# Linear attention feeding a routed expert layer: another route to 1/rms, routing logits summed on GpSimd, three routing groups for four

## Chip, cores and metric

One core of a Trainium2 chip runs the kernel. The metric is the device time of one execution in microseconds (us). TensorE does the matrix products and transposes (PE in the profile, PEld its weight loads), VectorE is DVE, ScalarE is ACT, GpSimd is POOL, and SyncE (SP) issues most loads. Each engine executes its instructions strictly in the order in which the kernel wrote them, and waits where an operand is not ready.

## What is computed

The reference, cut to what matters (q, k, v are 8 batches x 8 heads x 576 rows x 64; x is 4608 rows x 512; there are 8 experts of 512 x 1024 x 512):

```python
kv  = einsum('bhsd,bhde->...', k, v)          # one 64x64 state per batch and head
out = einsum('bhsd,bhde->bhse', q, kv)
rms = sqrt(mean(out * out, axis=-1) + 1e-06)  # per row and head
x   = (out / rms * g_norm)                    # -> (4608, 512)
do_compute = x @ w_skip > 0
logits = x[do_compute] @ w_gate; e_idx = argmax(logits)
gate_w = max softmax probability
out[do_compute] += gate_w * (relu(x @ w1[e]) @ w2[e])   # e = e_idx of the row
```

## The kernel before

There are two parts: an attention part, up to about 181 us in the trace, and an expert part after it.

**Units.** The 4608 rows are 36 tiles of 128. A *unit* is two tiles and four of the eight heads, so there are 36 units, and after unit n all of the tiles up to n are done. A batch gives four units; the ninth column of rows of four batches is collected into two more units, without a transpose of their own. Units 0 to 17 belong to batches 0 to 3 and 18 to 35 to batches 4 to 7.

**A step of the loop.** Step n of the main loop writes, in this order: `turn(n+1)` (four PE transposes of q, L287, and ACT's copy `qT` out of PSUM, L290); `values(n)` (32 matmuls into `o_ps`, L322, and ACT's Square of the result into `sq`, L327); the extra jobs of PE that are due in the step; `norm(n-1)` (DVE multiplies `o_ps` by 1/rms into `xl`, L344); `scale(n)` (DVE sums `sq` over the 64 columns into `rs`, L334, and POOL raises it to the power -1/2, L335); `finish(n-1)` (POOL multiplies by `g_norm` into `xb`, L362, and copies the nine logit columns into `lp`, L366); and the extra jobs of DVE. `o_ps` has two buffers, so `values(n+1)` waits for `xl` of unit n-1. The mean's 1/64 and the epsilon are folded into constants: `sq` has a 65th column that holds 64 times 1e-6, and `g_norm` is scaled by 8.

**The extra jobs on PE** prepare the state of a batch in the five steps ahead of its first unit: `state` twice (72 matmuls each, L219; the second ends with ACT's copy `kvn`, L226), `state_t` (transposes L235, ACT's copy `kvT` L238), `state_m` (the gating weights times the state, L246, two DVE copies L250), `state_s` (a product with a swap matrix L256, ACT's copy `kvs` L259). All use the one buffer of `kv_ps`, so the next batch's first `state` waits for `kvs`. `turn_8` (L302, two ACT copies L306) transposes the collected rows; it shares the one PSUM buffer of `turn`. With four units to a batch the steps repeat in a cycle of four, called here **A** (`state_s`, then the first `state` of the next batch), **B** (the second `state`), **C** (`turn_8`, `state_t`) and **D** (`state_m`).

**Logits.** The nine gating columns (eight experts and the skip score) are extra columns of the state, so each unit's `xl` holds 4 heads x 9 partial logits per row; a row's logits are their sum over the eight heads.

**Routing groups.** The tiles are routed in four groups that end after 8, 18, 26 and 36 tiles. For each: `choose` (DVE sums `lp` over the heads, L391, then finds the best expert, L394 to L409), `rank` (PE counts rows of equal expert, L419 to L427), `number` (DVE turns the counts into slot numbers, L436 to L447, builds one-hot rows `oha_k` of 128 columns per tile, L449, and `ohc` and `bv`, L457 and L461), and `settle` (PE, L470, and two DVE additions into `srow`, L482). Three groups are handled inside the loop, one to three steps apart; `early` then starts one indirect gather from the slots known so far. The last group of ten tiles is handled behind the loop, while PE works on the first rows of expert 0; there too ACT's `Exp` (L597) starts the chain of gate weights (L599 to L605, L457, L461, L470), which the remaining rows of expert 0 wait for.

**Expert part.** PE multiplies 384 rows per expert by w1 (L634) and w2 (L641), eight times; this takes PE alone from about 203 us to the end.

Of the kernel before, what the change touches and what calls it, by code (L numbers as in the profile page):

```python
# [7 lines left out]
FP32 = mybir.dt.float32  # L8
# [8 lines left out]
def kernel(  # L17
# [29 lines left out]
    nc = tc.nc  # L47
# [140 lines left out]
    nc.vector.tensor_copy(out=top[:, :], in_=ebase[:, :])  # L188


    sqs = [setup.tile([P, 2, 4, D + 1], FP32, name=f"sq{i}") for i in range(2)]
    for t in sqs:
        nc.vector.memset(t[:, :, :, D:D + 1], float(D * 1e-6))
    half_t = setup.tile([P, 2, 4], FP32)
    nc.vector.memset(half_t[:, :, :], -0.5)

# [75 lines left out]
    NU = len(units)  # L272
    ends = [8, 18, 26, 36]
    TG = 10

    qTs, q8s, ops, rss, lps, xbs = {}, {}, {}, {}, {}, {}

# [33 lines left out]
    def values(n):  # L311
        _, b, i, u = units[n]
        qT = qTs.pop(n)
        ps = ps_o.tile([P, 2, 512], FP32, tag="o", name="o_ps")
        for w in range(2):
            for a in range(2):
                for hf in range(2):
                    for r in range(2):
                        bb = b if i is not None else 4 * b + 2 * hf + r
                        rows = slice(r * 64, (r + 1) * 64)  # L320
                        kv = kvns[bb] if w == r else kvss[bb]
                        nc.tensor.matmul(  # L322
                            out=ps[hf * 64:(hf + 1) * 64, r, (2 * w + a) * KD:(2 * w + a + 1) * KD],
                            lhsT=qT[rows, w, hf, a * 64:(a + 1) * 64], rhs=kv[rows, a, u, :],
                            start=True, stop=True, skip_group_check=True)
        sq = sqs[n % 2]
        nc.scalar.activation(out=sq[:, :, :, 0:D], in_=heads(ps, 0, D), func=ACT.Square)  # L327
        ops[n] = (ps, sq)

    def scale(n):  # L330

        _, sq = ops[n]
        rs = att_pool.tile([P, 2, 4], FP32, tag="rs", name="rs")
        nc.vector.tensor_reduce(out=rs[:, :, :], in_=sq[:, :, :, :], axis=AX.X, op=ALU.add)  # L334
        nc.gpsimd.tensor_tensor(out=rs[:, :, :], in0=rs[:, :, :], in1=half_t[:, :, :], op=ALU.pow)  # L335
        rss[n] = rs

    def norm(n):

        nq, b, i, u = units[n]  # L340
        (ps, _), rs = ops.pop(n), rss.pop(n)
        r4 = rs[:, :, :].unsqueeze(3)
        xl = att_pool.tile([P, 2, 4, KD], FP32, tag="xl", name="xl")
        nc.vector.tensor_tensor(out=xl[:, :, :, :], in0=heads(ps, 0, KD),  # L344
# [3 lines left out]
    def finish(n, xl):  # L348
# [3 lines left out]
        if t0 == 0 and u == 0:  # L352
            lps[g] = gat_pool.tile([P, TG, H, G], FP32, tag="lp", name="lp")
        if i is None:
# [3 lines left out]
        else:  # L358
# [6 lines left out]
            in1=g_b[:, :].unsqueeze(1).unsqueeze(1).to_broadcast([P, 2, 4, D]), op=ALU.mult)  # L365
        nc.gpsimd.tensor_copy(out=lps[g][:, t0:t0 + 2, 4 * u:4 * u + 4, :], in_=xl[:, :, :, D:KD])  # L366
        if u == 0:
# [15 lines left out]

    ohbs, rks, bvs, sps = {}, {}, {}, {}

    def choose(g):
        t0, t1 = ([0] + ends)[g], ends[g]
        nt = t1 - t0
        lp = lps.pop(g)
        lg = gat_pool.tile([P, TG, G], FP32, tag="lg", name="lg")[:, 0:nt, :]  # L390
        nc.vector.tensor_reduce(out=lg, in_=lp[:, 0:nt, :, :].rearrange("p t h g -> p t g h"),  # L391
                                axis=AX.X, op=ALU.add)
        mx = gat_pool.tile([P, TG], FP32, tag="mx", name="mx")[:, 0:nt]
# [37 lines left out]
    def number(g):  # L431
# [16 lines left out]
                                       op=ALU.arith_shift_right)  # L448
        nc.vector.tensor_tensor(out=oha_k[:, t0:t1, :],  # L449
                                in0=row128_i[:, :].unsqueeze(1).to_broadcast([P, nt, P]),  # L450
                                in1=lo_i.unsqueeze(2).to_broadcast([P, nt, P]), op=ALU.is_equal)
        bvs[g] = columns(t0, nt, colid_i, row_k, 2, gat_pool)

    def columns(t0, nt, colid, val, pieces, pool):
# [104 lines left out]
    for n in range(NU + 2):  # L559
        if n + 1 < NU:  # L560
            turn(n + 1)
        if n < NU:
            values(n)
        jobs(n, "pe")
        done = norm(n - 1) if 1 <= n <= NU else None
        if n < NU:
            scale(n)
        store = done() if done else None
        if store:
            at(n + 1, "end", store)  # L570
        jobs(n, "dve")
        if n in ends[:LAST]:
# [3 lines left out]
            at(n + 1, "dve", lambda g=g: number(g))  # L576
            at(n + 2, "pe", lambda g=g: settle(g))
            at(n + 2, "dve", lambda g=g: add_pieces(srow[:, :], sps.pop(g), 2))
            if g == LAST - 1:
                at(n + 2, "dve", early)  # L580
        jobs(n, "end")
# [186 lines left out]
```

## Time and profile before

| | |
|---|---|
| runs | 547.68, 547.9, 550.95 us (median 547.9) |
| the profiled execution | 547.66 us, its span 545.9 us |
| mean granted PE clock | 0.92 |
| busy share of the span | PE 85%, DVE 23%, ACT 16%, POOL 31% |
| first Square of the loop | 29.26 us |
| last Square of the loop (unit 35) | 176.21 us |

A row of the group view reads: line, engine, operation, output <- inputs, shape, count | busy us in all, mean ns of one | idle us of that engine just before, and what ended the idling. A row of the windows view gives a stretch, its length, busy us of the engines with their instruction counts, the granted PE clock as a share of full speed, and the share of DMA. In the timeline a row gives start, duration, engine, line, operation, and in brackets the idle time before it and what ended it; in the chain of waits, start, duration, and the engine and line that time was spent on.

### The profile page before, as it was taken

How to read it: one execution, taken by the hardware profiler on the slowest of the kernel's cores; microseconds unless marked ns; L12 is line 12 of the kernel's file. 1: busy time of each engine (PE TensorE's matmuls, PEld its weight loads, DVE VectorE, ACT ScalarE, POOL GpSimd, SP SyncE). 2: the span in 40 equal slices, each digit the busy share in tenths (PEclk: the TensorE clock that was granted, in tenths of full speed). 3: DMA queues.
4: the chain of work that ended last, by engine and by line, in shares of the span. 5: the costliest groups of instructions: out<-in, count | busy, mean ns of one | idle time of the engine just before them, and what ended most of it. 6: DMA issues, size and time to landing. Idle time of an engine off the chain costs nothing.

```text
span 545.9 us, 8655 instructions
## 1 busy us (share of the span) xinstructions
PE 462.9 (85%) x3776; PEld 285.4 (52%) x3776; DVE 124.7 (23%) x265; ACT 89.8 (16%) x182; POOL 168.1 (31%) x183
## 2 busy tenths in 40 slices
PE   2477686867674789999999999999999999999990
PEld 2365565655553658455455455455445545545540
DVE  0223473383554670101101100110210210110011
ACT  0144433324332102011011011001001001101100
POOL 2038769757789467310100010010010010010010
PEclk9998958669865699999999999999999999999997
DMA  8997966779593446753241350431422000010000
GB/s 292 376 391 264 368 226 163 255 257 396 181 391 81 117 120 208 269 193 104 89 156 48 126 182 2 172 127 47 174 66 110 1 32 0 1 39 12 0 38 16
DMA packets 33226, 83.16 MB, mean 152 GB/s; under 512 B 3441, under 2 KB 3441, under 8 KB 33184
## 3 DMA queue, kind: packets, MB, share of 16 engines
q1 hardware_dynamic: 25216, 61.87, 31.6%
q0 software_dynamic: 5248, 15.92, 8.7%
q10 hardware_dynamic: 2720, 4.77, 3.4%
q8 instruction: 31, 0.51, 0.4%
q14 instruction: 11, 0.09, 0.1%
HBM read 68.21 MB, written 15.99 MB: 154 GB/s over the span
## 4 chain that ended last, share of the span: by engine, by line
PE 69%; DVE 12%; POOL 9%; issue 4%; DMA 4%; ACT 1%; POOLq 0%; DVEq 0%
PE hps L634 30%; PE yps L641 29%; POOL rs L335 6%; DVE rs L334 3%; DMA q<-in_q_dram 2%; PE o_ps L322 2%; DVE xl L344 2%; PE kv_ps L219 2%; DMA wraw<-in_moe_w_gate_dram 2%; PE q_ps L287 2%; PE xp L619 1%; POOL xb L362 1%; DVE xt L621 1%; DVE oha_k L449 1%; DVE ohc L457 1%
## 5 line engine op out<-in xcount | busy, mean ns | idle before, releaser
L634 PE MATMUL hps<-xt,w 128*128 128x384 f32 (+2 forms) x576 | 169.6, 456 | 4.3 <-DVE xt L621 4.3
L641 PE MATMUL yps<-w,ht 128*128 128x512 f32 x384 | 166.3, 592 | 0.0
L634 PEld LDWEIGHTS hps<-xt,w 128*128 128x128 f32 x576 | 106.5, 195 | 67.4 <-DVE xt L621 4.9
L641 PEld LDWEIGHTS yps<-w,ht 128*128 128x128 f32 x384 | 72.3, 190 | 87.8 <-issue 87.5
L651 POOL DMA_INDIRECT out_dram<-xg,rows x24 | 23.6, 985 | 288.0 <-DVE xg L648 273.9
L636 ACT ACTIVATE ht<-hps 128x384 f32<-128x384 f32 (+2 forms) x72 | 32.8, 456 | 303.0 <-PE hps L634 294.8
L335 POOL TENSOR_TENSOR rs<-rs,half_t 128x8 f32<-128x8 f32 x36 | 59.3, 1646 | 61.1 <-DVE rs L334 52.9
L648 DVE SCALAR_TENSOR_TENSOR xg<-yps,gate,xg 128x512 f32<-128x512 f32 x24 | 18.0, 751 | 161.7 <-PE yps L641 161.7
L621 DVE COPY xt<-xp 128x512 f32<-128x512 f32 x24 | 15.8, 687 | 137.0 <-PE xp L619 136.7
L322 PE MATMUL o_ps<-kvn,qT 64*64 64x73 f32 x512 | 31.4, 271 | 14.7 <-DVE xl L344 9.9
L362 POOL TENSOR_TENSOR xb<-xl,g_b 128x512 f32<-128x512 f32 x32 | 39.8, 1243 | 0.0
L344 DVE TENSOR_TENSOR xl<-o_ps,rs 128x584 f32<-128x584 f32 x36 | 27.6, 766 | 49.1 <-POOL rs L335 48.9
L219 PE MATMUL kv_ps<-v,k 64*64 64x64 f32 x1152 | 23.4, 240 | 17.0 <-DMA v<-in_v_dram 10.5
L322 PEld LDWEIGHTS o_ps<-kvn,qT 64*64 64x64 f32 x512 | 25.3, 168 | 22.7 <-issue 12.5
L322 PE MATMUL o_ps<-kvs,qT 64*64 64x73 f32 x512 | 30.9, 271 | 1.8 <-issue 1.8
L219 PEld LDWEIGHTS kv_ps<-v,k 64*64 64x64 f32 x1152 | 21.7, 154 | 20.5 <-issue 15.0
L287 PE MATMUL q_ps<-ident,q 128*128 128x128 f32 x128 | 27.1, 348 | 5.5 <-DMA q<-in_q_dram 4.1
L496 POOL DMA_INDIRECT xg<-out_dram,src x24 | 24.5, 1022 | 15.8 <-DVE src L491 8.9
L334 DVE TENSOR_REDUCE rs<-sq 128x8 f32<-128x520 f32 x36 | 24.7, 686 | 12.3 <-ACT sq L327 12.3
L327 ACT ACTIVATE sq<-o_ps 128x512 f32<-128x512 f32 x36 | 21.5, 598 | 35.8 <-PE o_ps L322 34.8
L290 ACT COPY qT<-q_ps 128x512 f32<-128x512 f32 x32 | 18.8, 586 | 52.5 <-PE q_ps L287 48.1
L322 PEld LDWEIGHTS o_ps<-kvs,qT 64*64 64x64 f32 x512 | 24.7, 168 | 1.9 <-issue 1.9
(105 smaller groups left out, 217.9 us busy)
## 6 DMA issues: line engine op xcount, KB each, us to landing
w<-in_moe_w_dram SPq DMA_DIRECT2D x16, 2048.0 KB, 9.6
k<-in_k_dram SPq DMA_DIRECT2D x8, 1152.0 KB, 10.9
v<-in_v_dram SPq DMA_DIRECT2D x8, 1152.0 KB, 14.2
q<-in_q_dram SPq DMA_DIRECT2D x8, 1152.0 KB, 12.4
out_dram<-xb POOLq DMA_DIRECT2D x8, 512.0 KB, 7.2
out_dram<-xb ACTq DMA_DIRECT2D x8, 512.0 KB, 6.5
out_dram<-x ACTq DMA_DIRECT2D x2, 256.0 KB, 3.2
out_dram<-x POOLq DMA_DIRECT2D x2, 256.0 KB, 3.6
```

The source lines that it names most:

```text
L219: nc.tensor.matmul(out=ps[w * 64:(w + 1) * 64, a, u * D:(u + 1) * D], lhsT=kt[r, 2 * u + w, c, :], rhs=vt[r, 2 * u + w, c, :], start=(c == ...
L287: nc.tensor.transpose(out=ps[:, w, hf, :], in_=qts[b][:, 2 * u + w, c:c + 2, :], identity=ident[:, :])
L322: nc.tensor.matmul(out=ps[hf * 64:(hf + 1) * 64, r, (2 * w + a) * KD:(2 * w + a + 1) * KD], lhsT=qT[rows, w, hf, a * 64:(a + 1) * 64], rhs ...
L334: nc.vector.tensor_reduce(out=rs[:, :, :], in_=sq[:, :, :, :], axis=AX.X, op=ALU.add)
L335: nc.gpsimd.tensor_tensor(out=rs[:, :, :], in0=rs[:, :, :], in1=half_t[:, :, :], op=ALU.pow)
L344: nc.vector.tensor_tensor(out=xl[:, :, :, :], in0=heads(ps, 0, KD), in1=r4.to_broadcast([P, 2, 4, KD]), op=ALU.mult)
L362: nc.gpsimd.tensor_tensor(out=xb[:, :, 4 * u * D:(4 * u + 4) * D].rearrange("p r (h d) -> p r h d", d=D), in0=xl[:, :, :, 0:D], in1=g_b[:, ...
L496: nc.gpsimd.indirect_dma_start(out=xg[:, c, :], out_offset=None, in_=out[0:upto, :], in_offset=bass.IndirectOffsetOnAxis(ap=src[:, col:col ...
L634: nc.tensor.matmul(out=hps[:, cols], lhsT=w_sb[e][0][:, dc, f * P:(f + 1) * P], rhs=xt[:, dc, cols], start=(dc == 0), stop=(dc == DC - 1))
L636: nc.scalar.activation(out=ht[:, f, cols], in_=hps[:, cols], func=ACT.Relu)
L641: nc.tensor.matmul(out=yps[:, :], lhsT=ht[:, f, c * P:(c + 1) * P], rhs=w_sb[e][1][:, f, :], start=(f == 0), stop=(f == FC - 1))
L651: ins = nc.gpsimd.indirect_dma_start(out=out[:, :], out_offset=bass.IndirectOffsetOnAxis(ap=rows[:, col:col + 1], axis=0), in_=xg[:, c, :] ...
```

## The change

Four things are changed.

1. **1/rms.** POOL's power goes. ACT takes the square root of `rs` with scale 1/64 and the epsilon as bias, right behind the Square in its own order, and DVE takes the reciprocal at the start of `norm`. The 65th column of `sq` and the scaling of `g_norm` go.
2. **Place of the PE jobs.** They are written behind `norm` and `scale` instead of ahead. PE's own order is unchanged by this, but the copies that the jobs give to ACT and DVE now stand behind the square root and behind the sum.
3. **Logits.** For every second unit POOL adds the two halves and then folds four heads to one (three additions), ahead of `xb`; the copy into `lp` (L366) and DVE's sum (L391) go.
4. **Groups** of 18, 8 and 10 tiles. For the first two, POOL builds the one-hot rows of one tile at a time, three or four tiles per step, so `settle` comes six and two steps later; DVE builds them only for the last group.

```diff
-    ends = [8, 18, 26, 36]
-    TG = 10
+    ends = [18, 26, 36]
+    TG = 18
...
     def scale(n):
         nc.vector.tensor_reduce(out=rs[:, :, :], in_=sq[:, :, :, :], axis=AX.X, op=ALU.add)
-        nc.gpsimd.tensor_tensor(out=rs[:, :, :], in0=rs[:, :, :], in1=half_t[:, :, :], op=ALU.pow)
+        nc.scalar.activation(out=rs[:, :, :], in_=rs[:, :, :], func=ACT.Sqrt, scale=1.0 / D,
+                             bias=eps_t[:, 0:1])
...
     def norm(n):
+        nc.vector.reciprocal(out=rs[:, :, :], in_=rs[:, :, :])
-        xl = att_pool.tile([P, 2, 4, KD], FP32, tag="xl", name="xl")
+        xl = att_pool.tile([P, 2, 4, KD], FP32, tag="xl", name="xl", bufs=4)
...
     def finish(n, xl):
+        if u == 0:
+            halves[nq] = xl
+        else:
+            lp = att_pool.tile([P, 2, 4, G], FP32, tag="lp", name="lp", bufs=2)
+            nc.gpsimd.tensor_tensor(out=lp[:, :, :, :], in0=halves.pop(nq)[:, :, :, D:KD],
+                                    in1=xl[:, :, :, D:KD], op=ALU.add)
+            nc.gpsimd.tensor_tensor(out=lp[:, :, 0:2, :], in0=lp[:, :, 0:2, :],
+                                    in1=lp[:, :, 2:4, :], op=ALU.add)
+            nc.gpsimd.tensor_tensor(out=lgs[g][:, t0:t0 + 2, :], in0=lp[:, :, 0, :],
+                                    in1=lp[:, :, 1, :], op=ALU.add)
...
-        nc.gpsimd.tensor_copy(out=lps[g][:, t0:t0 + 2, 4 * u:4 * u + 4, :], in_=xl[:, :, :, D:KD])
...
     def choose(g):
-        nc.vector.tensor_reduce(out=lg, in_=lp[:, 0:nt, :, :].rearrange("p t h g -> p t g h"),
-                                axis=AX.X, op=ALU.add)
+        lg = lgs.pop(g)[:, 0:nt, :]
...
+    def spread(g, lo, hi):
+        for t in range(lo, hi):
+            nc.gpsimd.tensor_scalar(out=oha_k[:, t, :], in0=row128_i[:, :],
+                                    scalar1=los[g][:, t - ([0] + ends)[g]:t - ([0] + ends)[g] + 1],
+                                    scalar2=None, op0=ALU.is_equal)
...
-        jobs(n, "pe")
         done = norm(n - 1) if 1 <= n <= NU else None
         if n < NU:
             scale(n)
+        jobs(n, "pe")
...
-            at(n + 2, "pe", lambda g=g: settle(g))
-            at(n + 2, "dve", lambda g=g: add_pieces(srow[:, :], sps.pop(g), 2))
+            t0, t1 = ([0] + ends)[g], n
+            per = 3 if g == 0 else 4
+            step = 2
+            for t in range(t0, t1, per):
+                at(n + step, "dve", lambda g=g, t=t: spread(g, t, min(t + per, ends[g])))
+                step += 1
+            at(n + step, "pe", lambda g=g: settle(g))
+            at(n + step, "dve", lambda g=g: add_pieces(srow[:, :], sps.pop(g), 2))
```

The diff does not tell how the instructions stand behind one another; three places follow. The first is ACT's queue over three steps of the loop, cycle steps C, D and A: before

```order
L290 COPY qT<-q_ps 128x512
L327 ACTIVATE sq_162<-o_ps 128x8x64
L306 COPY q_421<-q_ps 64x2x128
L306 COPY q_422<-q_ps 64x2x128
L238 COPY kvT<-kv_ps 64x512
L379 DMA out_dram<-xb 64x2x1024
L290 COPY qT<-q_ps 128x512
L327 ACTIVATE sq_161<-o_ps 128x8x64
L290 COPY qT<-q_ps 128x512
L327 ACTIVATE sq_162<-o_ps 128x8x64
L259 COPY kvs<-kv_ps 128x292
L290 COPY qT<-q_ps 128x512
```

and now, in steps A, B and C (L282 is `qT`, L319 the Square, L327 the square root, L251 `kvs`, L218 `kvn`, L298 `turn_8`'s copies, L230 `kvT`):

```order
L319 ACTIVATE sq<-o_ps 128x512
L327 ACTIVATE rs<-rs,eps_t 128x8
L251 COPY kvs<-kv_ps 128x292
L282 COPY qT<-q_ps 128x512
L319 ACTIVATE sq<-o_ps 128x512
L327 ACTIVATE rs<-rs,eps_t 128x8
L218 COPY kvn<-kv_ps 128x4x64
L282 COPY qT<-q_ps 128x512
L319 ACTIVATE sq<-o_ps 128x512
L327 ACTIVATE rs<-rs,eps_t 128x8
L298 COPY q_423<-q_ps 64x2x128
L298 COPY q_424<-q_ps 64x2x128
```

Between a Square and whatever ACT does next there now stands a square root, whose operand is DVE's sum of that Square. The second place is DVE's queue at the end of a group inside the loop: before (the group of ten tiles)

```order
L334 TENSOR_REDUCE rs<-sq_161 128x8
L391 TENSOR_REDUCE lg<-lp 128x90
L394 TENSOR_REDUCE mx<-lg 128x10
L396 TENSOR_SCALAR do<-lg 128x10
L398 TENSOR_TENSOR sh_k<-lg,mx 128x80
L402 SCALAR_TENSOR_TENSOR oh<-sh_k,eorder 128x80
L406 TENSOR_REDUCE fi<-oh 128x10
L407 TENSOR_TENSOR fi<-fi,do 128x10
L409 TENSOR_TENSOR ohb<-eorder,fi 128x80
L344 TENSOR_TENSOR xl<-o_ps,rs 128x584
L334 TENSOR_REDUCE rs<-sq_162 128x8
```

and now (the group of 18 tiles; L326 is the sum, L335 the reciprocal, L338 the product `xl`):

```order
L326 TENSOR_REDUCE rs<-sq 128x8
L395 TENSOR_REDUCE mx<-lg 128x18
L397 TENSOR_SCALAR do<-lg 128x18
L399 TENSOR_TENSOR sh_k<-lg,mx 128x144
L403 SCALAR_TENSOR_TENSOR oh<-sh_k,eorder 128x144
L407 TENSOR_REDUCE fi<-oh 128x18
L408 TENSOR_TENSOR fi<-fi,do 128x18
L410 TENSOR_TENSOR ohb<-eorder,fi 128x144
L335 RECIPROCAL rs<-rs 128x8
L338 TENSOR_TENSOR xl<-o_ps,rs 128x584
L326 TENSOR_REDUCE rs<-sq 128x8
```

The sum over the heads is gone from the front of the group's work. The third place is ACT's queue behind the loop: before

```order
L327 ACTIVATE sq_162<-o_ps 128x8x64
L379 DMA out_dram<-xb 64x2x1024
L373 DMA out_dram<-x_2340 64x2x512
L636 ACTIVATE ht<-hps 128x128 x8
L597 ACTIVATE ex<-sh_k 128x288
L636 ACTIVATE ht<-hps 128x256 x8
```

and now

```order
L327 ACTIVATE rs<-rs,eps_t 128x8
L383 DMA out_dram<-xb 64x2x1024
L377 DMA out_dram<-x_2428 64x2x512
L656 ACTIVATE ht<-hps 128x128 x8
L617 ACT_TABLE_LOAD
L617 ACTIVATE ex<-sh_k 128x288
L656 ACTIVATE ht<-hps 128x256 x8
```

A table load has appeared right ahead of the exponential. There is one more, at the first square root, and none behind the later ones.

More of the change, by code (lines that the diff above doesn't have):

```diff
@@ L325, in values @@
                             start=True, stop=True, skip_group_check=True)
-        sq = sqs[n % 2]
-        nc.scalar.activation(out=sq[:, :, :, 0:D], in_=heads(ps, 0, D), func=ACT.Square)
+        sq = att_pool.tile([P, 2, 4, D], FP32, tag="sq", name="sq", bufs=2)
+        nc.scalar.activation(out=sq[:, :, :, :], in_=heads(ps, 0, D), func=ACT.Square)
         ops[n] = (ps, sq)
@@ L448, in number @@
                                        op=ALU.arith_shift_right)
[L449 to L452 removed]
+        if g == len(ends) - 1:
+            nc.vector.tensor_tensor(out=oha_k[:, t0:t1, :],
+                                    in0=row128_i[:, :].unsqueeze(1).to_broadcast([P, nt, P]),
+                                    in1=lo_i.unsqueeze(2).to_broadcast([P, nt, P]),
+                                    op=ALU.is_equal)
+        else:
+            lo_f = gat_pool.tile([P, TG], FP32, tag="lo_f", name="lo_f")[:, 0:nt]
+            nc.vector.tensor_copy(out=lo_f, in_=lo_i)
+            los[g] = lo_f
+        bvs[g] = columns(t0, nt, colid_i, row_k, 2, gat_pool)
+    def spread(g, lo, hi):
[3 more added lines that the diff above has]
+                                    scalar2=None, op0=ALU.is_equal)
     def columns(t0, nt, colid, val, pieces, pool):
```

19 lines of the change are left out of this document (6 added, 13 removed).

## The prediction

> **What bounds the kernel now.** I read the page first, then the windows of the loop, then the timelines of POOL, DVE and ACT, and last the chain of waits for PE's pieces. In the page's groups the power on POOL stands out:
>
> ```profile
> L335 POOL TENSOR_TENSOR rs<-rs,half_t 128x8 f32<-128x8 f32 x36 | 59.3, 1646 | 61.1 <-DVE rs L334 52.9
> L344 DVE TENSOR_TENSOR xl<-o_ps,rs 128x584 f32<-128x584 f32 x36 | 27.6, 766 | 49.1 <-POOL rs L335 48.9
> ```
>
> Eight numbers per partition cost POOL 1.65 us, 36 times, and DVE sat idle for 48.9 us until they came, while POOL sat idle for 52.9 us until DVE's sum came. The two wait for each other in turn, and the timelines show one turn:
>
> ```profile
> 79.92 1.63 POOL L335 TENSOR_TENSOR rs<-rs,half_t 128x8 f32<-128x8 f32 x1
> 81.52 1.19 POOL L362 TENSOR_TENSOR xb<-xl,g_b 128x512 f32<-128x512 f32 x1
> ...
> 83.10 1.64 POOL L335 TENSOR_TENSOR rs<-rs,half_t 128x8 f32<-128x8 f32 x1 [0.21 <-DVE rs L334]
> ```
>
> ```profile
> 81.58 0.77 DVE L344 TENSOR_TENSOR xl<-o_ps,rs 128x584 f32<-128x584 f32 x1 [1.75 <-POOL rs L335]
> 82.27 0.68 DVE L334 TENSOR_REDUCE rs<-sq 128x8 f32<-128x520 f32 x1
> ```
>
> Power 1.63, product 0.69 (the sum starts 0.69 behind it), sum 0.68, hand-overs: 83.10 - 79.92 = 3.18 us per unit at the least, 114 us for 36 units. The loop takes more. I cut it at starts of Squares (29.26 is unit 0, 176.21 unit 35, 181.01 the last `xl`):
>
> ```profile
> 29.26:66.03 36.77, 26.40 (x793) 21.58 (x786) 12.59 (x21) 14.87 (x29) 25.46 (x25) 0.95 0.93 335
> 66.03:77.74 11.71, 8.21 (x113) 6.97 (x113) 9.75 (x26) 3.44 (x7) 6.07 (x7) 0.55 0.93 337
> 77.74:98.37 20.63, 15.58 (x371) 12.71 (x371) 8.59 (x14) 7.61 (x16) 18.35 (x20) 0.75 0.55 164
> 98.37:107.00 8.63, 8.13 (x219) 6.46 (x220) 2.83 (x4) 3.14 (x6) 6.99 (x8) 0.63 0.88 273
> 107.00:120.77 13.77, 8.53 (x119) 7.28 (x119) 10.58 (x26) 3.49 (x8) 7.67 (x8) 0.66 0.57 194
> 120.77:142.80 22.03, 16.89 (x525) 13.31 (x526) 8.77 (x14) 9.88 (x20) 18.64 (x20) 0.98 0.77 294
> 142.80:155.62 12.82, 8.26 (x113) 7.01 (x113) 10.10 (x29) 3.48 (x7) 7.17 (x8) 0.61 0.99 353
> 155.62:176.21 20.59, 11.46 (x210) 8.86 (x210) 8.20 (x12) 6.28 (x12) 19.54 (x21) 0.58 0.61 201
> 176.21:181.01 4.80, 1.08 (x4) 0.71 (x4) 1.37 (x2) 0.60 (x1) 4.67 (x6) 0.50 0.32 67
> ```
>
> Columns: stretch, its length, busy us of PE, PEld, DVE, ACT and POOL, granted clock, DMA share, GB/s. They are steps 0-8, 9-10, 11-16, 17-18, 19-20, 21-26, 27-28, 29-34, and the end. The second, fifth and seventh hold two steps each around a group's handling, and take 11.7 to 13.8 us for what should take about 6.4.
>
> **The new ring.** With the square root on ACT, ACT's strict order makes a new circle: Square, DVE's sum, square root, then the copies of the step's PE job, then the next `qT`, then the next Square. PE's pieces at full clock (from 42.41) and at half clock (from 100.07), in the chain of waits:
>
> ```profile
> 42.41 1.28 PE kv_ps L219 x72
> 43.69 0.59 PE q_ps L287 x4
> 44.27 0.67 PE o_ps L322 x32
> ...
> 100.07 2.20 PE kv_ps L219 x72
> 102.27 1.04 PE q_ps L287 x4
> 103.31 1.23 PE o_ps L322 x32
> ```
>
> ACT's durations and DVE's reciprocal have near relations:
>
> ```profile
> L327 ACT ACTIVATE sq<-o_ps 128x512 f32<-128x512 f32 x36 | 21.5, 598 | 35.8 <-PE o_ps L322 34.8
> L290 ACT COPY qT<-q_ps 128x512 f32<-128x512 f32 x32 | 18.8, 586 | 52.5 <-PE q_ps L287 48.1 <-PE o_ps L322 2.1 <-POOL lp L366 2.1
> L306 ACT COPY q<-q_ps 64x256 f32<-64x256 f32 x16 | 5.1, 366 | 0.5 <-PE q_ps L302 0.4
> L226 ACT COPY kvn<-kv_ps 128x256 f32<-128x256 f32 x8 | 3.0, 376 | 18.4 <-PE kv_ps L219 18.4
> L636 ACT ACTIVATE ht<-hps 128x128 f32<-128x128 f32 x5 | 1.4, 277 | 11.9 <-DMA out_dram<-xb 8.2 <-PE hps L634 3.6
> L601 DVE RECIPROCAL gw<-gw 128x36 f32<-128x36 f32 x1 | 0.4, 378 | 0.0
> ```
>
> ACT grows by 0.32 us from 128 to 512 columns, so eight columns cost about 0.18 by the line through both; no less than nothing, no more than the 0.28 of 128 columns. I take 0.20. The reciprocal lies between nothing and the 0.38 of 36 columns; I take 0.20, as it has fewer than a quarter of the columns. Each hand-over I put at 0.05 us. The circle without a job is then 0.60 + 0.05 + 0.68 + 0.05 + 0.20 + 0.59 + 0.05 = about 2.25 us, and DVE's own circle (reciprocal, product, sum, trip to ACT) 0.20 + 0.69 + 0.68 + 0.35 = 1.95.
>
> The moved jobs cost more than that. Before, `kvs` came right behind the Square, and a step of kind A took 3.71 us:
>
> ```profile
> 135.60 0.60 ACT L327 ACTIVATE sq<-o_ps 128x512 f32<-128x512 f32 x1 [0.95 <-PE o_ps L322]
> 136.25 0.40 ACT L259 COPY kvs<-kv_ps 128x292 f32<-128x292 f32 x1
> ...
> 139.31 0.60 ACT L327 ACTIVATE sq<-o_ps 128x512 f32<-128x512 f32 x1
> ```
>
> Now the sum and the square root stand between, 0.68 + 0.20 + two hand-overs = about 1.0, and PE's next `state` waits for `kvs` behind them: **A** is 4.7 us. **B** is the circle and `kvn` (0.38): 2.65. **C**: `turn_8`'s two copies (0.37 each, 0.65 together as they overlap a little) end 2.25 behind the Square, and only then may PE transpose again and do the values: 2.25 + 0.59 + 0.67 + 0.1 = 3.6. **D** is 2.3; DVE's `kvn` copies fit ahead of its product. A batch: 4.7 + 2.65 + 3.6 + 2.3 = 13.25 us; before it was 129.80 to 142.80 = 13.0 by the starts of Squares. The removed power is eaten by the ring: **in the undisturbed cycle I expect no gain at all.**
>
> **Stretch by stretch** (now against before):
>
> - Steps 0-8: A, B, C, D as above, with both stalls of PE inside (2.4 and 3.2 us of "issue" in the chain): 36.2 for 36.8, -0.6.
> - Steps 9-10 lose their group: C + D = 5.9 for 11.7, -5.8.
> - Steps 11-16 have little PE work and were set by the power: 2.7 + 2.3 + 3.6 + 2.1 + 2.25 + 2.3 = 15.2 for 20.6, -5.4.
> - Steps 17-18: A + B = 7.4 for 8.6, -1.2.
> - Steps 19-20 now have the group of 18. What each group paid before:
>
> ```profile
> L391 DVE TENSOR_REDUCE lg<-lp 128x72 f32<-128x576 f32 x2 | 2.3, 1172 | 6.3 <-POOL lp L366 6.3
> L449 DVE TENSOR_TENSOR oha_k<-row_i,lo_i 128x1024 bf16<-128x1024 int32 x2 | 2.5, 1226 | 0.0
> ```
>
>   With eight tiles 3.15 us of waiting for POOL's last `lp`, 1.2 for the sum over heads, 1.2 for the one-hot rows (with ten a quarter more): all three leave DVE. Of DVE's 10.58 busy us in these two steps, products and sums are 2.9, heads and one-hot rows 3.0; about 4.7 stays. With 18 tiles it is between 4.7 and 8.5 (in proportion); I take 5.4, since most of these operations are so short that their start outweighs their columns: 1.9 for `choose`, 3.5 for `number`. `rank` puts 36 matmuls on PE behind C's own; `number` starts some 3.4 us behind Square 19, ends at 6.9, and `xl`, sum, root and `qT` follow: 9.3 for 13.8, -4.5 (at worst 3 less).
> - Steps 21-26: 4.7 + 4.9 (with its 2.2 us of PE stall) + 3.6 + 2.3 + 4.7 + 3.6 (with `settle`) = 23.8 for 22.0, +1.8.
> - Steps 27-28, group of 8: 7.5 for 12.8, -5.3.
> - Steps 29-34: 2.7 + 2.5 + 3.6 + 3 x 1.95 = 14.65 for 20.6, -5.9.
> - The end: Square to last `xl` 0.60 + 0.68 + 0.20 + 0.20 + hand-overs = 1.85 for 4.8, -2.95.
>
> Sum: -29.85 us with PE at full clock.
>
> **Behind the loop** the chain of waits goes through ACT:
>
> ```profile
> 193.20 0.28 ACT ht L636
> 193.48 0.34 ACT ex L597
> ```
>
> The change puts a table load between the two. The one in the trace:
>
> ```profile
> L226 ACT ACT_TABLE_LOAD x1 | 1.3, 1283 | 3.8 <-issue 3.8
> ```
>
> +1.3 us, not hidden, since all gate weights follow it. (The first square root's load stands while ACT waits for the sum.) `choose` of the last group starts 2.7 us earlier, but PE's work ahead of `rank` sets the time there; I count nothing, at best -2. The Trainium skill, "ScalarE: Activation LUTs", section "What ACT_TABLE_LOAD costs", adds about 1.38 us of draining to a load of 1.28; by it the sum would be 1.4 us higher. The trace shows the load's 1283 ns and no drain apart from it.
>
> **PE's clock.** At half clock A costs 0.92 + 0.45 + 0.56 = 1.9 more, C 1.0; B and D become PE's own: 2.20 + 1.04 + 1.23 = 4.5, and for D, whose eight matmuls I put at 1.9, 4.2. That is 1.7 us more per step with a job. Before, the rows above show 0.55 to 0.75 in five stretches. It fell after thin stretches:
>
> ```profile
> 87.50:90.90 3.40, 1.39 (x36) 1.00 1.00 222
> 90.90:94.30 3.40, 1.83 (x36) 0.52 0.94 281
> ```
>
> The new ring leaves PE no pause over 1.4 us in the cycle, but step 20 does, and step 28 with little after it. I charge one spell of 13.6 us in steps 20-23, as long as those seen, and part of a second: about five steps x 1.7 = +8. The Trainium skill, "TensorE: Matmul & The Clock Gate", section "Part 1: The HAM clock gate", makes an idle window of about 3.4 us the condition; by it I would charge only step 20. The row disagrees in part: 1.39 busy us of 3.4 were enough.
>
> **POOL** goes from a power, an `xb` and a copy per unit (3.18 us with hand-overs, above) to `xb` and half of three small additions, which at a quarter of `xb` each make 1.6 in all. One-hot rows add three per step for six steps, then four for two. `is_equal` on 128 columns is not in the trace on POOL:
>
> ```profile
> L114 POOL IOTA row_i<- 128x128 int32 x1 | 0.2, 226 | 0.4 <-POOLq L754 0.4
> ```
>
> From 0.23 (an iota of that size) to 1.65 (the power); I take 0.4, a third of the 1.19 of `xb`, which has four times the columns: 1.2 to 1.6 us per step, inside steps of 3.3. At 1.65 each, eight steps would take 6.5 to 8 on POOL and about 25 us would come on the path.
>
> **Total:** -29.85 + 1.3 + 8 = -20.5 against the profiled 547.66 us (span 545.9, 1.8 around it), which lies 0.2 below the median: **527 us**.
>
> **Rivals.** (1) *Dearer trips through ACT.* If root, reciprocal and hand-overs cost 0.45 us more per unit than I think, 36 x 0.45 = 16 come back: 543 us. For it: none of the three is in the trace; against it: 0.28 and 0.38 bound them. (2) *PE stays at half clock*, the slower side: A 6.6, B 4.5, C 4.6, D 4.2 = 19.9 a batch for 13.25, +50 over seven and a half batches in place of my 8: 569 us. It decides once more than some 60% of the steps run so, where the gain of 28.5 is used up. For it: 0.50 to 0.66 in four stretches before; against it: those followed stalls of which most go, and PE, when it is the limit itself, is busy throughout and regained full clock after 104.5. (3) *POOL becomes the bound* through dear one-hot rows: 527 + 25 = 552 us; against it, the ramp from 0.23. (4) *The change does not do what it says*, a table load at every Square and root, 72 x 1.28 = +92: the instruction order shows one load only.
>
> **Chances.** Forecast 0.80, (1) 0.11, (2) 0.05, (3) 0.04, (4) 0. The forecast's own range is 517 (no cold spell, -2 behind the loop) to 541: 18 cold steps, as about half were before, would be 18 x 1.7 = 31 for my 8, so 550; I go half that way, to 538, and add 3 for a dearer root or `number`. I give 516 to 541, which leaves out the upper half of (1), and (2) and (3). A measurement can tell about 1% from no change. Faster by more than that: the forecast, and a third of (1) and (3): 0.85; within: most of the rest of both: 0.09; slower: (2) and the worst of (3): 0.06.
>
> **What would show it.** Right: a step A near 4.7 us from Square to Square, C near 3.6, a batch cycle no shorter than 13; two steps around a group at 7 to 9.5; the last steps near 2; no wait of DVE for POOL's `lp`; a table load of 1.28 just ahead of the exponential. Wrong: a cycle clearly under 13 (then ACT's ring is not the limit), a clock near 0.5 through the loop, POOL ahead of DVE in the waits, or steps 11-16 still at 3.2.

## The result, and the profile after

The change took 531.35 us (median of 4, 526.54 to 536.72) where the kernel before, run beside it, took 549.42 (547.68 to 552.36): a ratio of 0.9637, 95% interval 0.9538 to 0.9735. Ratios leave out runs that lie over 1.5% above the fastest of the same kernel (here the one of 536.72 us, later one run each of `four_groups` and `root_order`), while medians and ranges include them. Its profiled execution took 529.38 us, with a span of 527.5 and a mean granted clock of 0.937.

The same cuts at starts of Squares, now of the change (29.00 is unit 0, 159.26 unit 35, 161.28 the last `xl`; columns as in the prediction):

```profile
29.00:65.58 36.58, 25.73 (x797) 21.29 (x790) 15.49 (x31) 18.11 (x40) 15.07 (x23) 0.98 0.95 335
65.58:74.11 8.53, 6.87 (x87) 5.60 (x85) 3.70 (x8) 3.97 (x9) 2.67 (x5) 0.64 1.01 350
74.11:92.29 18.18, 13.75 (x371) 11.33 (x372) 10.14 (x20) 9.08 (x21) 10.74 (x18) 0.88 0.78 254
92.29:101.21 8.92, 7.95 (x218) 6.27 (x218) 3.33 (x9) 3.39 (x9) 3.07 (x6) 0.64 0.79 264
101.21:109.14 7.93, 6.16 (x125) 5.39 (x126) 7.44 (x23) 3.75 (x10) 2.23 (x5) 0.99 0.51 135
109.14:133.33 24.19, 18.99 (x543) 15.23 (x543) 11.03 (x26) 11.00 (x27) 21.96 (x36) 0.86 0.85 327
133.33:142.73 9.40, 7.80 (x105) 6.69 (x105) 7.15 (x23) 3.96 (x9) 4.92 (x9) 0.66 0.93 329
142.73:159.26 16.53, 9.75 (x218) 7.40 (x218) 10.36 (x23) 7.84 (x18) 13.24 (x22) 0.81 0.85 332
159.26:161.28 2.02, 1.09 (x4) 0.72 (x4) 1.45 (x3) 0.90 (x2) 1.70 (x3) 0.50 0.03 8
```

The lengths add up to 132.28 us where before they gave 151.75: 19.5 us came out of the loop. Behind it, from the last `xl` to the end of the span, stand 366.2 us for 364.9. The groups of instructions that answer to those of before:

```profile
L327 ACT ACTIVATE rs<-rs,eps_t 128x8 f32<-128x8 f32 x36 | 10.8, 301 | 31.3 <-DVE rs L326 31.3
L335 DVE RECIPROCAL rs<-rs 128x8 f32<-128x8 f32 x36 | 7.3, 202 | 9.7 <-ACT rs L327 9.4
L338 DVE TENSOR_TENSOR xl<-o_ps,rs 128x584 f32<-128x584 f32 x36 | 27.6, 767 | 4.3 <-POOL oha_k L463 0.5
L463 POOL TENSOR_SCALAR oha_k<-row_i,lo_f 128x128 bf16<-128x128 int32 x26 | 15.2, 598 | 0.0
```

DVE's product `xl` cost the same 767 ns, but the idle time ahead of it fell from 49.1 us to 4.3, and the wait of DVE for the power is gone. What took its place is the circle through ACT, here over one step of kind A (Square 41.06 to Square 45.71):

```profile
41.06 0.60 ACT L319 ACTIVATE sq<-o_ps 128x512 f32<-128x512 f32 x1
42.41 0.30 ACT L327 ACTIVATE rs<-rs,eps_t 128x8 f32<-128x8 f32 x1 [0.75 <-DVE rs L326]
42.61 0.38 ACT L251 COPY kvs<-kv_ps 128x292 f32<-128x292 f32 x1
44.95 0.58 ACT L282 COPY qT<-q_ps 128x512 f32<-128x512 f32 x1 [1.96 <-PE q_ps L279]
45.71 0.60 ACT L319 ACTIVATE sq<-o_ps 128x512 f32<-128x512 f32 x1 [0.17 <-PE o_ps L314]
```

ACT waits 0.75 us for DVE's sum, takes the root, and only then copies `kvs`, for which PE's next `state` stands. 4.65 us from Square to Square, as forecast at 4.7.

### The profile page after: what moved, and what is told of

Its sections match the earlier page's. It is cut to its first block, busy times and chain, and to the rows that moved or that the text cites. A ratio compares the mean times of both kernels' runs of the same rounds, so it can differ in the third digit from the quotient of the medians.

```text
span 527.5 us, 8703 instructions
## 1 busy us (share of the span) xinstructions
PE 455.6 (86%) x3776; PEld 279.9 (53%) x3776; DVE 120.9 (23%) x274; ACT 100.3 (19%) x220; POOL 129.3 (25%) x191
## 4 chain that ended last, share of the span: by engine, by line
PE 76%; DVE 9%; DMA 4%; ACT 3%; POOL 3%; issue 2%; ACTq 1%; DVEq 0%
PE hps L654 31%; PE yps L661 30%; PE o_ps L314 4%; PE q_ps L279 3%; PE kv_ps L211 2%; DVE rs L326 2%; DMA q<-in_q_dram 2%; PE kv_ps L238 2%; DMA wraw<-in_moe_w_gate_dram 2%; ACT sq L319 2%; PE xp L639 1%; DVE xl L338 1%; POOL xb L367 1%; DVE xt L641 1%; POOL oha_k L463 1%
## 5 line engine op out<-in xcount | busy, mean ns | idle before, releaser
L367 POOL TENSOR_TENSOR xb<-xl,g_b 128x512 f32<-128x512 f32 x32 | 37.9, 1184 | 47.9 <-DVE xl L338 47.9
L211 PE MATMUL kv_ps<-v,k 64*64 64x64 f32 x1152 | 24.5, 247 | 19.2 <-DMA v<-in_v_dram 10.5
L279 PE MATMUL q_ps<-ident,q 128*128 128x128 f32 x128 | 25.2, 330 | 17.9 <-ACT q L298 11.3
L326 DVE TENSOR_REDUCE rs<-sq 128x8 f32<-128x512 f32 x36 | 24.6, 684 | 49.2 <-ACT sq L319 48.8
L211 PEld LDWEIGHTS kv_ps<-v,k 64*64 64x64 f32 x1152 | 22.8, 161 | 22.7 <-issue 13.4
L314 PE MATMUL o_ps<-kvn,qT 64*64 64x73 f32 x512 | 29.0, 255 | 3.4 <-issue 2.8
L314 PE MATMUL o_ps<-kvs,qT 64*64 64x73 f32 x512 | 27.9, 255 | 1.5 <-issue 1.2
L338 DVE TENSOR_TENSOR xl<-o_ps,rs 128x584 f32<-128x584 f32 x36 | 27.6, 767 | 4.3 <-POOL oha_k L463 0.5
L314 PEld LDWEIGHTS o_ps<-kvn,qT 64*64 64x64 f32 x512 | 23.1, 154 | 10.2 <-issue 5.4
L279 PEld LDWEIGHTS q_ps<-ident,q 128*128 128x128 f32 x128 | 16.7, 165 | 22.0 <-ACT q L298 12.9
L319 ACT ACTIVATE sq<-o_ps 128x512 f32<-128x512 f32 x36 | 21.5, 597 | 15.0 <-PE o_ps L314 14.4
L282 ACT COPY qT<-q_ps 128x512 f32<-128x512 f32 x32 | 18.6, 582 | 28.0 <-PE q_ps L279 27.6
L314 PEld LDWEIGHTS o_ps<-kvs,qT 64*64 64x64 f32 x512 | 22.2, 154 | 1.8 <-issue 1.4
## 6 DMA issues: line engine op xcount, KB each, us to landing
v<-in_v_dram SPq DMA_DIRECT2D x8, 1152.0 KB, 12.4
```

What stands on the lines that cost most here:

```text
L211: nc.tensor.matmul(out=ps[w * 64:(w + 1) * 64, a, u * D:(u + 1) * D], lhsT=kt[r, 2 * u + w, c, :], rhs=vt[r, 2 * u + w, c, :], start=(c == ...
L279: nc.tensor.transpose(out=ps[:, w, hf, :], in_=qts[b][:, 2 * u + w, c:c + 2, :], identity=ident[:, :])
L314: nc.tensor.matmul(out=ps[hf * 64:(hf + 1) * 64, r, (2 * w + a) * KD:(2 * w + a + 1) * KD], lhsT=qT[rows, w, hf, a * 64:(a + 1) * 64], rhs ...
L319: nc.scalar.activation(out=sq[:, :, :, :], in_=heads(ps, 0, D), func=ACT.Square)
L367: nc.gpsimd.tensor_tensor(out=xb[:, :, 4 * u * D:(4 * u + 4) * D].rearrange("p r (h d) -> p r h d", d=D), in0=xl[:, :, :, 0:D], in1=g_b[:, ...
```

## The experiments

In all that follows a ratio is to the kernel before, run in the same rounds on the same chip. The second set (the four from `four_groups` to `cheap_power`) ran on a chip on which everything behind the loop takes 377 to 380 us for 365 to 367, the kernel before 564.71 us in all, so that only its ratios and loops bear comparing, not its times.

**root_only**: before, with the root and the reciprocal and nothing else. Four groups, PE jobs ahead of the sum, logits and one-hot rows on DVE stay.

```diff
-        nc.gpsimd.tensor_tensor(out=rs[:, :, :], in0=rs[:, :, :], in1=half_t[:, :, :], op=ALU.pow)
+        nc.scalar.activation(out=rs[:, :, :], in_=rs[:, :, :], func=ACT.Sqrt, scale=1.0 / D,
+                             bias=eps_t[:, 0:1])
...
+        nc.vector.reciprocal(out=rs[:, :, :], in_=rs[:, :, :])
```

> The kernel before with one edit: square root on ScalarE and reciprocal on VectorE in place of GpSimd's power; four groups, the copy and VectorE's sum over heads, and the PE jobs ahead of norm and scale all stay. My theory (the root buys nothing in the undisturbed batch cycle, since ScalarE's ring is as long as the GpSimd round trip, and gains only where steps are thin, at a group's wait for the last logits and at the end): about 534 us, with a batch cycle of 13 to 14 us from Square to Square. Rival 1 (the round trip of 3.18 us is replaced by 2.25 us in every step): 515 us. Rival 2 (the gain of the change is all in the groups and logits): 546 us or more.

529.6 us (528.49 to 531.62), ratio 0.9642 [0.96, 0.9683]: all of the gain of the whole change, 0.9637, and 4 us less than the 534 that I had expected. The two steps around each group (9-10, 19-20, 27-28), with all the group's work still on DVE:

```profile
66.83:76.00 9.17, 5.55 (x111) 4.63 (x110) 8.54 (x29) 3.75 (x9) 2.71 (x4) 0.89 1.00 367
102.37:111.32 8.95, 6.42 (x119) 5.58 (x119) 8.39 (x25) 3.82 (x10) 2.76 (x4) 0.82 0.65 222
137.88:147.30 9.42, 6.40 (x113) 5.38 (x113) 8.79 (x33) 3.82 (x9) 2.73 (x4) 0.73 0.98 334
```

9.2, 9.0 and 9.4 for 11.7, 13.8 and 12.8 before, and for 8.5, 7.9 and 9.4 in the change, which has no group at the first place. So most of what a group cost came with the power. Two rows show how. The wait of DVE's sum over heads for POOL, by the table of waits of before and then of `root_only` (total, times, longest):

```profile
DVE lg L391 <- POOL lp L366: 10.7, 4, 3.2
```

```profile
DVE lg L388 <- POOL lp L363: 0.9, 1, 0.9
```

POOL made `lp` late since the power and `xb` stood ahead of it. Three of before's four waits, 9.4 us in all, fall into the loop. Then DVE's one-hot columns in before's first group, and POOL's work at that time:

```profile
73.08 1.34 DVE L457 TENSOR_TENSOR ohc<-colid_i,hi_k 128x192 bf16<-128x192 int32 x1
...
72.51 1.70 POOL L362 TENSOR_TENSOR xb<-xl,g_b 128x512 f32<-128x512 f32 x1
```

The same instruction in `root_only`, where POOL was busy for 2.7 to 2.8 us of each of the three stretches:

```profile
L454 DVE TENSOR_TENSOR ohc<-colid_i,hi_k 128x192 bf16<-128x192 int32 x2 | 0.7, 349 | 0.0
```

0.35 us for 1.34: in before, `ohc` ended 0.21 us behind the end of `xb` (72.51 + 1.70 = 74.21), as if it had had to wait for it. The Trainium skill, "SBUF — State Buffer", section "SBUF: two separate sides", says that a DVE operation with two SBUF inputs and a GpSimd one that reads SBUF share a pair of ports as an exclusive lock; the two rows agree with that, though no run here takes the lock apart. In the loop's three groups `ohc` fell from 4.08 us to 1.10 in all; with the 8.5 us less of waiting for `lp` that is 11.5 us, about the 10.8 by which the stretches shrank. PE's clock was higher as well, 0.89, 0.82 and 0.73 for 0.55, 0.66 and 0.61, and PE was busy for 18.4 us in the three for 25.0; what part of the 10.8 that would explain is not separated.

**power_kept**: the whole change, but with the power on POOL.

```diff
-        nc.scalar.activation(out=rs[:, :, :], in_=rs[:, :, :], func=ACT.Sqrt, scale=1.0 / D,
-                             bias=eps_t[:, 0:1])
+        nc.gpsimd.tensor_tensor(out=rs[:, :, :], in0=rs[:, :, :], in1=half_t[:, :, :], op=ALU.pow)
...
-        nc.vector.reciprocal(out=rs[:, :, :], in_=rs[:, :, :])
```

> The changed kernel with GpSimd's power put back in place of root and reciprocal; three groups, logits and one-hot rows on GpSimd and the moved jobs stay. My theory: without the root the rest is worth nothing, since GpSimd then has 1.65 + 1.19 + 0.4 us per unit and 1.8 to 2.4 us of one-hot rows on top in eight steps, and becomes the bound there: about 550 us, with those eight steps near 5 us. Rival (the groups and logits carry the gain, the root none): 535 us.

552.96 us (552.28 to 554.69), ratio 1.0066 [1.0031, 1.0101]: slower than before by a little. One group less in the loop, and what left DVE, bring nothing without the root; steps 21-26 and 29-34 become POOL's:

```profile
112.42:144.31 31.89, 23.19 (x543) 18.28 (x544) 8.85 (x16) 9.78 (x20) 31.08 (x41) 0.71 0.72 260
...
154.61:180.50 25.89, 13.87 (x218) 10.32 (x218) 8.64 (x17) 6.38 (x13) 24.20 (x30) 0.57 0.41 131
```

POOL is busy for 31.08 of 31.89 us and 24.20 of 25.89. Its timeline shows one step of 4.5 us:

```profile
126.50 1.77 POOL L467 TENSOR_SCALAR oha_k<-row_i,lo_f 128x128 bf16<-128x128 int32 x3
128.25 1.67 POOL L333 TENSOR_TENSOR rs<-rs,half_t 128x8 f32<-128x8 f32 x1
129.89 1.17 POOL L371 TENSOR_TENSOR xb<-xl,g_b 128x512 f32<-128x512 f32 x1
```

1.77 + 1.67 + 1.17: a one-hot row costs 0.6 us, three of them as much as the power that the root takes away. This is rival (3) in a kernel in which it holds.

**jobs_first**: the change, with PE's jobs again ahead of the product and the sum.

```diff
+        jobs(n, "pe")
         done = norm(n - 1) if 1 <= n <= NU else None
         if n < NU:
             scale(n)
-        jobs(n, "pe")
```

> The changed kernel with the PE jobs written ahead of norm and scale again, as before the change. By the instruction orders: step A falls from 4.65 to about 3.7 us (the swapped state's copy no longer waits for the root), C from 3.8 to 3.35, B stays, D rises from 2.25 to about 3.95 (VectorE's two copies wait for PE ahead of the product). My theory, that these orders set the steps: 533 us, about no difference. Rival (the move is what made the change pay): 545 us or more.

531.81 us (528.41 to 533.27), ratio 0.9668 [0.9617, 0.9719], no different from the change. Undisturbed steps, read from starts of Squares: A 3.60 for 4.65, C 2.76 for 3.82, but D 3.71 to 3.83 for 2.25. So the new place of the jobs makes A and C about 1.05 us longer each and D about 1.5 shorter, and its sum over the whole program can't be told from nothing.

**exp_early**: the change, and a one-column exponential right behind the loop, so that the table load comes where ACT has nothing to do.

```diff
+    warm = keep.tile([P, 1], FP32)
+    nc.scalar.activation(out=warm[:, :], in_=ident[:, 0:1], func=ACT.Exp)
     assert not todo
```

> The changed kernel with one exponential of a single column added on ScalarE right behind the loop, so that the table is loaded there and no longer ahead of the exponential that starts the gate weights. My theory: the time from the last product of the loop to the end falls from 366.2 to about 364.9 us, the value of the kernel before. Rival (the load is hidden or its place does not matter): 366.2 us.

One run, 533.5 us. The part behind the loop went from 366.2 to 365.15. ACT around the exponential, in the change and then here:

```profile
173.55 0.28 ACT L656 ACTIVATE ht<-hps 128x128 f32<-128x128 f32 x1 [1.37 <-PE hps L654]
173.84 1.28 ACT L617 ACT_TABLE_LOAD   x1
175.13 0.44 ACT L617 ACTIVATE ex<-sh_k 128x288 f32<-128x288 f32 x1
```

```profile
170.19 1.28 ACT L603 ACT_TABLE_LOAD   x1 [4.01 <-POOL x L367]
...
178.99 0.28 ACT L658 ACTIVATE ht<-hps 128x128 f32<-128x128 f32 x1 [1.35 <-PE hps L656]
179.16 0.43 ACT L619 ACTIVATE ex<-sh_k 128x288 f32<-128x288 f32 x1
```

From `ht` to `ex` 1.58 us with the load between, 0.17 without it. The loop of this kernel is the change's own, and took 137.64 us in this execution, for 132.28 and (below) 131.99: a single profile's loop is known to some 5 us only, and the verdicts below rest on the timed ratios.

**four_groups**: the change with groups of 8, 10, 8 and 10 tiles, as before.

```diff
-    ends = [18, 26, 36]
-    TG = 18
+    ends = [8, 18, 26, 36]
+    TG = 10
```

> The changed kernel with the four groups of before (8, 10, 8 and 10 tiles) in place of three; root, logits and one-hot rows as in the change. My first reading (a group costs several us of VectorE and PE time, so leaving one out saved most of 5.8 us): 536 us. Reading after the root-only run (with the root a group's steps cost about as much as other steps, and the number of groups is worth nothing): 531 us.

Ratio 0.9678 [0.9632, 0.9724], loop 138.44. The interval of the change (0.9538 to 0.9735) covers this one: a group less is worth nothing that these runs can show.

**swap_first** and **swap_turn_first**: the change, with the job `state_s` (the first), or `state_s` and `turn_8` (the second), put back ahead of the product and the sum. Their copies then come ahead of the root on ACT, while D's `kvn` copies stay behind. The second has both edits:

```diff
-                at(max(n - 5 + i, 0), "pe", lambda b=b, part=part: part(b))
-        at(n + 1, "pe", lambda b=b: turn_8(b))
+                at(max(n - 5 + i, 0), "first" if part is state_s else "pe", lambda b=b, part=part: part(b))
+        at(n + 1, "first", lambda b=b: turn_8(b))
...
+        jobs(n, "first")
         done = norm(n - 1) if 1 <= n <= NU else None
```

> The changed kernel with one PE job, the swapped state, written ahead of norm and scale again, so that ScalarE copies it ahead of the square root; all other jobs stay behind. If ScalarE's order sets step A as predicted, A falls from 4.65 to about 3.65 us in five steps and the time by 5 us, to 526 us. If something else sets it (PE or VectorE), A stays at 4.65 and the time at 531 us.

> As swap_first, and also the transposes of the collected rows ahead of norm and scale. If ScalarE's order sets step C too, C falls from 3.8 to about 2.9 us in eight steps: with A a batch cycle of 11.5 us in place of 13.4, and about 519 us. If not, the time of swap_first.

`swap_first`: ratio 0.9669 [0.9627, 0.971], not to be told from the change; A fell to 3.72 in step 3, 3.60 in step 21 and 4.49 in step 7. `swap_turn_first`: ratio 0.9525 [0.9485, 0.9564], loop 128.18, about half of the further gain that was expected. A step of kind A on its ACT:

```profile
39.86 0.60 ACT L319 ACTIVATE sq<-o_ps 128x512 f32<-128x512 f32 x1
40.46 0.40 ACT L251 COPY kvs<-kv_ps 128x292 f32<-128x292 f32 x1
41.21 0.30 ACT L327 ACTIVATE rs<-rs,eps_t 128x8 f32<-128x8 f32 x1 [0.35 <-DVE rs L326]
```

The copy lies in the time in which ACT waited for the sum, and the step takes 4.01 us, to the Square at 43.87, for 4.65 (two later ones 4.49, where 3.65 was expected); C fell to 2.62 to 3.35. Step 30 took 6.29 us, where the profile of the change has 2.16. The chain of waits there:

```profile
139.79 2.32 POOL oha_k L463 x4
...
142.15 0.22 PE slot_ps L483
```

PE stands at `settle` for the last one-hot rows, four to a step on POOL. This does not come from the shorter steps alone: `exp_early`, whose loop is the change's own, took 6.24 us in its step 30, by the same chain:

```profile
149.65 2.32 POOL oha_k L463 x4
...
152.01 0.21 PE slot_ps L483
```

`four_groups` (6.35) and `jobs_first` (6.64) have it too. In the change's own profile PE came to `settle` late, after steps at half clock, and waited only 0.35 us for the last rows.

**cheap_power**: before, with the power replaced by an instruction on POOL that writes a constant. It leaves out the division by the rms; the trip DVE-POOL-DVE and before's order stay.

```diff
-        nc.gpsimd.tensor_tensor(out=rs[:, :, :], in0=rs[:, :, :], in1=half_t[:, :, :], op=ALU.pow)
+        nc.gpsimd.tensor_scalar(out=rs[:, :, :], in0=rs[:, :, :], scalar1=0.0, scalar2=0.66, op0=ALU.mult, op1=ALU.add)
```

> The kernel before with GpSimd's power replaced by one cheap GpSimd operation that writes the constant 0.66 (so the division by the rms is left out; sums, waits and engines stay). It prices the power alone, with no trip through ScalarE. If the trip through ScalarE takes back part of what the power cost, as predicted for the batch cycle: 519 us, with D at 2.3 to 2.4 us. If the trip is free and the power's 1.65 us were all: 529 us, the time of the root-only kernel.

```profile
L335 POOL TENSOR_SCALAR rs<-rs 128x8 f32<-128x8 f32 x36 | 7.1, 197 | 93.3 <-DVE rs L334 80.3 <-DVE srow L482 12.9
```

Ratio 0.9579 [0.9541, 0.9617], between the two expectations. With 0.2 us in place of 1.65 on the same engine the gain is there without any trip through ACT: the price of the power was the cost, not the engine's place in the circle. D was 3.09 where I had expected 2.3, and this says more than the ratio. Squares of an undisturbed batch, steps C and D of before (its A, 135.60 to 139.31, stands in the prediction), then C, D, A and the end of A here:

```profile
129.80 0.60 ACT L327 ACTIVATE sq<-o_ps 128x512 f32<-128x512 f32 x1 [2.60 <-PE o_ps L322]
132.51 0.60 ACT L327 ACTIVATE sq<-o_ps 128x512 f32<-128x512 f32 x1
```

```profile
120.52 0.60 ACT L327 ACTIVATE sq<-o_ps 128x512 f32<-128x512 f32 x1 [1.84 <-PE o_ps L322]
123.22 0.60 ACT L327 ACTIVATE sq<-o_ps 128x512 f32<-128x512 f32 x1
126.31 0.60 ACT L327 ACTIVATE sq<-o_ps 128x512 f32<-128x512 f32 x1 [0.96 <-PE o_ps L322]
130.03 0.60 ACT L327 ACTIVATE sq<-o_ps 128x512 f32<-128x512 f32 x1
```

2.70, 3.09 and 3.72 us for 2.71, 3.09 and 3.71: with the power gone and no trip through ACT in its place these steps stay as they were, so the power did not set them. Of the 22.2 us by which this loop is shorter (129.55 for 151.75), 9.0 lie in the three stretches around groups and 16.9 in steps 11-16, 29-34 and the end; the other stretches grew by 3.6. Against `root_only` (0.9642) the intervals touch, so what the trip through ACT costs beyond a cheap one through POOL lies somewhere from nothing to 1.4%.

**after_again**, the change itself, and **root_order**: `root_only` with all PE jobs but `state_s` and `turn_8` moved behind the product and the sum, that is `swap_turn_first` without the three groups and without what moved to GpSimd. Its edits are those of `root_only` together with the order of `swap_turn_first`.

> The changed kernel once more, on the chip and in the rounds of the two below, since chips differ. About 0.965 of the time of before.

> The kernel before with root and reciprocal, and with the swapped state and the transposes of the collected rows ahead of norm and scale and all other PE jobs behind; four groups, and logits and one-hot rows on VectorE as before. If root and order are all that counts and groups, logits and one-hot rows on GpSimd are worth nothing: the ratio of the kernel with the same order and all the rest of the change, 0.9525, within 0.005. If the rest of the change is worth its 15 us of my prediction: 0.97 or more.

The change 531.42 us (528.75 to 534.96), ratio 0.969 [0.9649, 0.9732]; `root_order` 524.31 (522.95 to 531.41), ratio 0.953 [0.9493, 0.9566], loop 127.65. With `swap_turn_first` at 0.9525 this is the second pair, after `root_only` and the change, in which groups, logits and one-hot rows together are worth nothing that can be measured. The order of the jobs is worth 1% or a little more: `root_order` lies under `root_only` (0.9642 [0.96, 0.9683]), which has all jobs ahead, and under the change run beside it, which has all of them behind, by intervals that lie apart.

**spread_early**: `swap_turn_first` with `exp_early`'s line, and the one-hot rows begun a step earlier.

```diff
-            step = 2
+            step = 1
...
+            step += 1
             at(n + step, "pe", lambda g=g: settle(g))
```

> The changed kernel with the swapped state and the transposes of the collected rows ahead of norm and scale, the exponential's table loaded right behind the loop, and GpSimd's one-hot rows started one step earlier with settle at the same step. In the trace of the kernel without the last two, settle of the second group waits for GpSimd's one-hot rows at step 30, which takes 6.3 us. If this wait is on the path: step 30 falls to 3 to 4 us, and with 1.1 us from the table the time is 3 to 4 us below that kernel, a ratio near 0.946. If GpSimd's rows cost nothing: 0.951.

522.69 us (519.64 to 526.81), ratio 0.9513 [0.9469, 0.9557], the value that I had named for rows that cost nothing. Step 30 did fall from 6.29 to 3.30, and the part behind the loop took 365.9 (`root_order` on the same chip 366.8), but the time is not to be told from `root_order` or `swap_turn_first`. In this profile the gather stands on the chain of waits; it was issued 8.6 us ahead of the loop's last `xl`, in `swap_turn_first` 11.6:

```profile
147.50 8.54 DMA xg<-out_dram,src
```

It is the fastest median of all, by a margin that the intervals do not resolve.

## Why the time came out as predicted, and where the reason was wrong

- *The power bounds the kernel before.* Right for the time, and shown by three runs: `root_only` (0.9642) and `cheap_power` (0.9579) have the gain, `power_kept` (1.0066) has none. It is not right for every step: it binds around the groups, in the thin steps and at the end, but not in the undisturbed batch, as the Squares of `cheap_power` show.
- *The new ring; "in the undisturbed cycle I expect no gain at all".* The lengths were right. A 4.65 (forecast 4.7), C 3.82 (3.6), D 2.25 (2.3); B was 2.37 and 3.13 in two steps (2.65) and 3.79 to 4.99 in three others, and steps 23 to 26 made a cycle of 13.85 us for 13.0 before. The order of ACT's copies sets A and C, as `swap_turn_first` shows by undoing it. The reason given, "The removed power is eaten by the ring", was not right: the power had not set these steps (`cheap_power`), so there was nothing to eat. Before, D's product waited behind the two `kvn` copies of DVE, and these for PE (2.42 us at 133.54). With the jobs moved behind, D falls by 0.84, and A and C rise, by 0.94 and 1.11.
- *The thin steps.* Right in kind: 11-16 took 18.2 for 20.6 (forecast 15.2), 29-34 took 16.5 for 20.6 (14.65), the end 2.02 for 4.80 (1.85). The root alone did at least as much here: in `root_only` the same three took 16.9, 14.2 and 2.02.
- *The three group stretches, -15.6 together.* The sum was near (-12.4: 8.53, 7.93 and 9.40 for 11.71, 13.77 and 12.82), the cause was not. The step that failed is "all three leave DVE" and "lose their group". In `root_only` nothing leaves DVE and no group goes, and the stretches still shrink by 10.8 (9.17, 8.95, 9.42). I had read the wait for `lp` and the long DVE work of a group as the group's own price; both came for the most part from a POOL that the power kept behind. What the move gains is lost elsewhere: `after_again` did take 5.92 in steps 9-10 (forecast 5.9), but 34.7 in steps 11-16 and 29-34 where `root_only` took 31.1, and its whole loop was only 2 us under that of `root_only` (131.99 and 134.19), less than one execution differs from the next.
- *Root 0.20 and reciprocal 0.20.* 0.301 and 0.202. The root lies above the 0.28 that I had taken as its upper bound from the activation of 128 columns; yet the ring's own steps came out no longer than forecast (A 4.65 for 4.7, D 2.25 for 2.3), so other terms of it were put too high by as much. The line through two wider activations missed what a column of bias costs: the Trainium skill, "ScalarE: Activation LUTs", section "What ACT_TABLE_LOAD costs", gives 280 ns + 0.833 ns per element for an activation with a bias column, 287 ns for eight; the row's 301 is near that.
- *One-hot rows 0.4 each, hidden.* 0.598 each. Steps 21-26 of the change came near the forecast (24.19 for 23.8), with POOL busy for 21.96 us of them. At `settle` in step 30 the rows were not hidden in four other runs (6.2 to 6.6 us), one of them with the change's own loop, and with the power (`power_kept`) POOL sets the steps. This is rival (3) in part.
- *The table load +1.3.* Right to a tenth: 366.2 for 364.9. The forecast left out the Trainium skill's further 1.38 us of draining, from the same section; the rows above show `ex` 0.01 us behind the load's end, and all in all 1.41 us more from `ht` to `ex`, so here it was right to leave it out.
- *The clock, +8.* The loop took 132.28 where the full-clock sum made 121.8: 10.5 for 8. Steps 17 and 21 (A, 6.55 as forecast for half clock) and 10 and 28 (D, 4.04 for 4.2) alone carry 2 x 1.9 + 2 x 1.8 = 7.4. Where the clock fell in the change (columns: stretch, length, PE busy, clock, DMA share, GB/s):

```profile
63.60:67.00 3.40, 1.33 (x11) 1.00 0.95 287
67.00:70.40 3.40, 2.60 (x39) 0.65 1.06 363
70.40:74.00 3.60, 3.60 (x44) 0.50 1.00 364
```

  In a step of kind C, PE's next transposes wait for Square, sum, root and `turn_8`'s copies. "The new ring leaves PE no pause over 1.4 us in the cycle" was right for the undisturbed C (1.40 us of waiting, ended at 53.07). Here it was 1.66 us, ended at 67.80, and a stall of 1.22 ("issue" in the chain of waits, from 63.58) stood just ahead: 1.33 busy us of 3.4 were left, much as the 1.39 before, and the clock fell. What the forecast had left out is a stall and a ring's pause that fall together, and a thin step: in step 15 PE waited 2.71 us, ended at 86.99, the 3.4 us from 85.00 were 41% busy, and the clock was 0.51 after that. The forecast had put its cold steps at 20-23 and 28. The trace has them in 9-10, 16-17, 21 and 28-29, so that a sum of 10.5 for 8 is in part luck. The rule of the Trainium skill that the prediction cited, an idle window of about 3.4 us, would have charged step 20 alone; steps 19-20 ran at 0.99, and two cold stretches here lie behind windows that were 39% and 41% busy. My windows need not be the chip's.

Not settled: why PE's stalls ("issue" in the chain), and with them the cold spells, fall at other steps in each execution (the change's runs go from 526.54 us at a mean clock of 0.945 to 536.72 at 0.915); what part of the groups' shrinking is the clock's; whether `swap_first` alone gains; and the trip through ACT against a cheap one through POOL.

## What to carry to other kernels

Eight numbers can cost more than 512 (here 1.65 us for the power, 1.18 for `xb`): look for the small instruction with a long mean in a circle of waits, and price it away first, by itself. A stretch that is long beside a slow engine may be long because of that engine; what its own work costs is only seen once the slow one is gone, and a step that keeps its length without the slow instruction was never set by it; so run the single edit before crediting the rest of a change. When an engine takes on a link of the ring, put the copies that others wait for into the time in which it waits, ahead of the link.

## What the runs showed of the hardware

- The power on POOL costs 1.65 us for 8 columns, a multiply-add by constants on the same tile 0.197 us.
- Comparing 128 columns of int32 with a number and writing bf16 took POOL 0.598 us, half of the 1.18 of `xb`, a product of 512 columns of f32.
- A one-column activation took 0.20 us (`warm`, in the timeline of `exp_early`), one of eight columns with a bias column 0.301.
